# Batch 0's queries and keys loaded as bf16 from POOL's queue, and a new order of the opening

## The chip, the core and the metric

The kernel runs on one core of one Trainium2 chip. A core has a matrix engine (TensorE, PE in the profile, with its weight loads as PEld), a vector engine (VectorE, DVE), an activation engine (ScalarE, ACT), GpSimd (POOL) and a queue engine (SyncE, SP) that here only issues DMAs. POOL issues DMAs as well; the DMAs that it issues may change the type of the data on the way. Each engine runs its own instructions in order and waits for others by semaphores. Sixteen DMA engines serve all queues. SBUF is the on-chip memory of 128 partitions; PSUM holds TensorE's results.

The metric is the device time of one execution in microseconds (us), median over runs.

## The reference

Sliding-window attention (window 32 to each side) over 8 batches of 8 heads, 576 positions, head size 64, and then a two-layer network with a leaky ReLU over the 4608 tokens:

```python
scores = scale * np.matmul(q, k.transpose(0, 1, 3, 2))
mask = np.abs(pos[:, None] - pos[None, :]) <= window
scores = np.where(mask, scores, -1000000000.0)
scores = scores - np.max(scores, axis=-1, keepdims=True)
attn = np.exp(scores)
attn = attn / (np.sum(attn, axis=-1, keepdims=True) + 1e-09)
attn_out = np.matmul(attn, v)

x = attn_out.transpose(0, 2, 1, 3).reshape(B * S, H * D)   # 4608 x 512
h = x @ w_in                                               # 512 x 2048
out = np.maximum(0.01 * h, h) @ w_out                      # 2048 x 512
```

All inputs and the output are float32; the kernel computes in bf16 with float32 sums.

## The kernel before

The eight heads of a batch are taken in four pairs, a pair filling the 128 partitions with 2 x 64. A batch's 576 positions are two halves of 288. A *step* is one pair of one half: step i belongs to batch i // 8, half (i // 4) % 2 and pair i % 4.

For a step, `score(i)` (from line 270) multiplies the transposed queries `qT` with blocks of keys `kbd` on TensorE, five matmuls into the one PSUM tile `ps`; ACT takes the exponential `e`; POOL multiplies it with the window's mask into `prob` (line 282). `kbd` and `vbd` hold a pair's keys or values as block-diagonal tiles: the two heads of a pair stand on their own partitions, zero elsewhere, so these tiles have to be cleared once. `sums(i)` adds the probabilities with a matmul with `ones_bd` and takes the reciprocal on DVE (line 309). `product(i)` multiplies `prob` with `vbd` into the PSUM tile `x`, and `scaled(i)` writes `x` times the reciprocal into `xT` (DVE, line 334). `x` and the sums' tile `s` have one buffer each.

Once the four pairs of a half are in `xT`, the network's tiles run: `h_tile` (four matmuls over the 128-row slices c of `w_in`, line 348, and the leaky ReLU on ACT) and `o_tile` (sixteen matmuls with `w_out`, line 390). For the first half of batch 0, `h_first` runs the matmuls slice by slice, so that slice c waits only for pair c; its last part, c = 3, waits for `scaled(3)`. These matmuls are the dense stream that fills most of the span. From `h_tile(0, 4)` on the order is laid out by hand until the second half of batch 1 begins, and then by a fixed plan of due times. Every `step` of batch 1 needs `vbd` of batch 1, cast on ACT from `vf` (`cast_v`, line 203).

How queries and keys get transposed differs by batch. Batch 0 and 1: SP loads `qf` and `kf` as float32 (`load_qk`, line 79: 96 partitions, 6 positions in a row in each, both heads of the pair), an engine casts them to bf16 into `qb` and `kb` (`cast_qk`, lines 195 and 197; the tile holds both heads of a position side by side), TensorE transposes them in 6 matmuls for a pair (`transposes`, line 225), ACT evicts the PSUM tile `tp` into `qT` (line 233) or `kT` (line 239), and DVE copies `kT` into `kbd` in two halves (`place_keys`, line 258). Later batches are transposed by DMA.

The opening is one list of calls at the end of the kernel. Its queues are these:

- SP: all loads of batch 0 in the order q and k of pair 0, of pair 1, values of pair 0, q and k of pairs 2 and 3, values of pairs 1 to 3. After them come the loads of batch 1, whose first one waits for a POOL memset (line 75).
- POOL: the identity, the window (a memset and four selections), the clear of `vbd` of pair 3, then casts of keys, the masks, casts of values of pair 0, the probabilities, and the eight weight loads (`load_w_in`, line 448, and `load_w_out`, line 452: each reads 1 MB of float32 and writes 512 KB of bf16).
- DVE: cast of the identity, constants, the clear of `kbd` (line 134), then casts of queries, placing of keys, reciprocals and scalings.
- ACT: clears of `vbd` of pairs 0 to 2 (line 127), evictions, exponentials, the cast of the queries of pair 3, and the casts of values of pairs 1 to 3.
- TensorE: transposes of pairs 0 and 1, scores 0 and 1, sums 0, transposes of pair 2, product 0, and so on. `keep_busy` (line 402) puts matmuls in between whose result nobody reads.

Of the kernel before, what the change touches and what calls it, by code (L numbers as in the profile page):

```python
# [9 lines left out]
FP32 = mybir.dt.float32  # L10
BF16 = mybir.dt.bfloat16
AF = mybir.ActivationFunctionType
# [4 lines left out]
def kernel(  # L17
# [69 lines left out]
    def load_v(b, p):  # L87

        t = fload.tile([128, NB, D], FP32, name=f"vf{p}")
        for a in range(2):  # L90
            nc.sync.dma_start(  # L91
                out=t[64 * a:64 * a + 64],
                in_=v[b, 2 * p + a].rearrange("(c p) d -> p c d", p=64),
            )
        vf[b, p] = t

    load_qk(0, 0)
    load_qk(0, 1)
    load_v(0, 0)
    load_qk(0, 2)  # L100
    load_qk(0, 3)
    for p in range(1, NPAIR):
        load_v(0, p)


    ident_f = const.tile([128, 128], FP32)
    make_identity(nc, ident_f)
    ident = const.tile([128, 128], BF16)
    nc.vector.tensor_copy(out=ident, in_=ident_f)
# [7 lines left out]
    qb = const.tile([96, NPAIR, RUN, 2, D], BF16)  # L117
    kb = const.tile([96, NPAIR, RUN, 2, D], BF16)

    kbd = [const.tile([128, NPAIR, NB, 128], BF16, name=f"kbd{i}") for i in range(2)]  # L120
    vbd = [const.tile([128, NPAIR, NB, 128], BF16, name=f"vbd{i}") for i in range(2)]
    zero = const.tile([128, 1], BF16)
    nc.vector.memset(zero, 0.0)
# [10 lines left out]
    nc.vector.memset(kbd[0], 0.0)  # L134
    clear(vbd[0], 0)
    clear(vbd[0], 1)
    clear(vbd[0], 2)


# [6 lines left out]
    win = const.tile([128, 2, 3, 64], BF16)  # L146
    nc.gpsimd.memset(win, 1.0)
    for lo in (0, 64):
        w = win[lo:lo + 64]
        nc.gpsimd.affine_select(  # L150
            out=w, in_=w, compare_op=ALU.is_ge, fill=0.0,
            base=0, channel_multiplier=-1, pattern=[[1, 2], [0, 3], [2, 64]],
        )
        nc.gpsimd.affine_select(
            out=w, in_=w, compare_op=ALU.is_ge, fill=0.0,
            base=2 * W, channel_multiplier=1, pattern=[[-1, 2], [0, 3], [-2, 64]],
        )
    nc.gpsimd.memset(vbd[0][:, 3], 0.0)
# [16 lines left out]
    )  # L175

# [22 lines left out]
    def cast_v(b, p, on_act=False):  # L199
        for a in range(2):  # L200
            r = slice(64 * a, 64 * a + 64)
            if on_act:
                nc.scalar.activation(out=vbd[b % 2][r, p, :, r], in_=vf[b, p][r], func=AF.Copy)  # L203
            else:
                nc.gpsimd.tensor_copy(out=vbd[b % 2][r, p, :, r], in_=vf[b, p][r])  # L205
# [11 lines left out]

    def transposes(b):

        qT[b] = attn.tile([128, NPAIR, S], BF16, name="qT")  # L220
        for p in range(NPAIR):
            for which, src in (("q", qb), ("k", kb)):
                tp = mmps.tile([128, RUN, 96], BF16, name="tp", tag="mm")
                for c in range(RUN):
                    nc.tensor.transpose(  # L225
                        tp[:, c],
                        src[:, p, c].rearrange("p a d -> p (a d)"),
                        ident[0:96, 0:96],
                    )

                tok = tp.rearrange("p (e c) i -> p c i e", c=2)
                if which == "q":
                    nc.scalar.activation(
                        out=qT[b][:, p].rearrange("p (c i e) -> p c i e", c=2, e=RUN // 2),
                        in_=tok, func=AF.Copy,
                    )
                else:
                    kT = kt.tile([128, S], BF16, name="kT")
                    nc.scalar.activation(  # L239
                        out=kT.rearrange("p (i c) -> p i c", c=RUN),  # L240
                        in_=tp.rearrange("p c i -> p i c"), func=AF.Copy,
                    )
                    unplaced.append((b, p, kT))
                yield
# [50 lines left out]
    def sums(i):  # L295
# [3 lines left out]
        s = xps.tile([128, HALF], FP32, name="s")  # L299
# [154 lines left out]
    first = transposes(0)  # L454

    def first_pair():
        next(first)
        next(first)
        place_keys()

    cast_qk(0, 0, nc.vector)
    make_mask(0)
    cast_qk(0, 1, nc.vector)
    first_pair()
    first_pair()
    cast_v(0, 0)
    score(0)
    cast_qk(0, 2, nc.vector)
    score(1)
    sums(0)  # L470
    next(first)
    next(first)
    product(0)
    keep_busy(ps, 0, 2)
    place_keys()
    cast_qk(0, 3, nc.scalar)
    load_w_in(0, 512)
    scaled(0)
    sums(1)
    keep_busy(ps, 0, 3)  # L480
    load_w_in(512, 1024)
    load_w_in(1024, 1536)
    next(first)
    score(2)
    next(first)
    cast_v(0, 1, on_act=True)
    load_w_in(1536, 2048)
    make_mask(1)
    place_keys()
    keep_busy(ps, 0, 8)  # L490
    sums(2)
    score(3)
    load_w_out(0)
    product(1)
    scaled(1)
    cast_v(0, 2, on_act=True)
# [7 lines left out]
    cast_v(0, 3, on_act=True)  # L504
# [87 lines left out]
    def spend(us):  # L592
        nonlocal clock, turn
        while due and due[0] <= clock + 1e-6:
            due.pop(0)
            i = state["done"]
            if i < 11:
                cast_v(1, i - 7, on_act=True)
            step()
            if 10 <= i < 14:  # L600
                load_v(2, i - 10)
# [5 lines left out]
        if turn == 4:  # L607
            second_pair(3)
            cast_v(1, 0, on_act=True)
# [37 lines left out]
```

## Time and profile before

| what | value |
|---|---|
| median of 3 runs | 319.77 us (318.51 to 320.29) |
| span of the profiled execution | 318.5 us |
| TensorE busy | 303.2 us, 95% of the span |
| DVE, ACT, POOL busy | 218.2, 182.6, 191.6 us |
| TensorE busy from 0 to 25 us | 14.1 of 25.0 us |
| TensorE busy from 25 to 60 us | 33.8 of 35.0 us |
| TensorE busy from 60 us to the end | 255.3 of 258.5 us |
| granted TensorE clock in every stage | 1.00 |

The rows by stage are sums over windows of the span. The median of the runs lies 1.27 us above the span of the profiled execution. The next lines are what the profile shows of the loads of the first 50 us: what is loaded, from which queue, how often, the size written, and the median time from issue to landing.

```profile
qf<-in_q_dram SPq DMA_DIRECT2D x8, 288.0 KB, 7.9
kf<-in_k_dram SPq DMA_DIRECT2D x8, 288.0 KB, 8.9
w_in_bf<-in_moe_w_in_dram POOLq DMA_DIRECT2D x4, 512.0 KB, 8.6
w_out_bf<-in_moe_w_out_dram POOLq DMA_DIRECT2D x4, 512.0 KB, 16.8
vf<-in_v_dram SPq DMA_DIRECT2D x12, 144.0 KB, 8.2
```

### The profile page before, as it was taken

How to read it: one execution, taken by the hardware profiler on the slowest of the kernel's cores; microseconds unless marked ns; L12 is line 12 of the kernel's file. 1: busy time of each engine (PE TensorE's matmuls, PEld its weight loads, DVE VectorE, ACT ScalarE, POOL GpSimd, SP SyncE). 2: the span in 40 equal slices, each digit the busy share in tenths (PEclk: the TensorE clock that was granted, in tenths of full speed). 3: DMA queues.
4: the chain of work that ended last, by engine and by line, in shares of the span. 5: the costliest groups of instructions: out<-in, count | busy, mean ns of one | idle time of the engine just before them, and what ended most of it. 6: DMA issues, size and time to landing. Idle time of an engine off the chain costs nothing.

```text
span 318.5 us, 6474 instructions
## 1 busy us (share of the span) xinstructions
PE 303.2 (95%) x2449; PEld 204.3 (64%) x2449; DVE 218.2 (69%) x259; ACT 182.6 (57%) x393; POOL 191.6 (60%) x251
## 2 busy tenths in 40 slices
PE   2679998999999999999999999999999999999996
PEld 1467774585765858576765858576665858576653
DVE  5678955869655997688755997688745988565100
ACT  7577698474652828374652828375552837464531
POOL 7798963974546866686546866586637866330000
PEclk9999999999999999999999999999999999999999
DMA  8999999997999995399735995399733430000101
GB/s 179 211 186 218 267 250 203 250 206 181 216 242 196 231 206 150 82 251 203 155 76 127 238 227 136 75 223 232 162 76 104 109 70 33 35 35 2 66 31 71
DMA packets 108400, 49.46 MB, mean 155 GB/s; under 512 B 68816, under 2 KB 103888, under 8 KB 108368
## 3 DMA queue, kind: packets, MB, share of 16 engines
q1 hardware_dynamic: 104144, 44.84, 66.8%
q0 software_dynamic: 4224, 4.19, 8.0%
q8 instruction: 19, 0.31, 0.4%
q14 instruction: 13, 0.11, 0.1%
HBM read 36.70 MB, written 9.44 MB: 145 GB/s over the span
## 4 chain that ended last, share of the span: by engine, by line
PE 89%; DMA 3%; DVE 2%; SPq 1%; POOL 1%; ACT 1%; issue 1%; DVEq 0%; ACTq 0%
PE mm L348 39%; PE mm L390 38%; PE x L320 5%; PE ps L275 4%; DMA kf<-in_k_dram 3%; PE s L301 2%; DVE r L309 2%; SPq L79 1%; POOL w_in_bf L448 1%; DVE xT L334 1%; PE tp L225 1%; PE s L304 1%; ACT vbd L203 0%; SPq L91 0%; POOL prob L282 0%
## 5 line engine op out<-in xcount | busy, mean ns | idle before, releaser
L309 DVE RECIPROCAL r<-s 128x288 f32<-128x288 f32 x64 | 125.2, 1956 | 56.5 <-PE s L301 53.3
L282 POOL TENSOR_TENSOR prob<-e,mask 128x576 bf16<-128x576 bf16 x64 | 81.5, 1274 | 87.8 <-ACT e L280 41.1
L348 PE MATMUL mm<-xT,w_in_bf 128*128 128x288 bf16 x1024 | 134.0, 286 | 0.3
L390 PE MATMUL mm<-w_out_bf,gT 128*128 128x512 bf16 (+2 forms) x592 | 130.4, 373 | 0.2 <-DMA w_out_bf<-in_moe_w_out_dram 0.2
L355 ACT ACTIVATE gT<-mm 128x288 bf16<-128x288 f32 x256 | 101.4, 412 | 24.8 <-PE mm L348 8.5
L348 PEld LDWEIGHTS <-w_in_bf 128*128 128x128 bf16 x1024 | 98.4, 98 | 24.8 <-issue 0.6
L390 PEld LDWEIGHTS <-gT 128*128 128x128 bf16 x592 | 56.3, 98 | 59.6 <-issue 0.3
L395 ACT ACTIVATE o_sb<-mm 128x512 f32<-128x512 f32 (+2 forms) x37 | 21.7, 586 | 92.0 <-PE mm L390 92.0
L280 ACT ACTIVATE e<-ps 128x576 bf16<-128x576 f32 x64 | 41.4, 648 | 9.4 <-PE ps L275 9.2
L197 POOL CAST kb<-kf 96x384 bf16<-96x384 f32 (+1 forms) x56 | 35.5, 656 | 4.6 <-DMA kf<-in_k_dram 4.6
L205 POOL CAST vbd<-vf 64x576 bf16<-64x576 f32 x50 | 34.5, 689 | 1.8 <-DMA vf<-in_v_dram 0.4
L334 DVE TENSOR_TENSOR xT<-x,r 128x288 bf16<-128x288 f32 x64 | 29.3, 458 | 8.2 <-PE x L320 1.2
L260 DVE COPY kbd<-kT 64x576 bf16<-64x576 bf16 x48 | 32.3, 672 | 0.3
L275 PE MATMUL ps<-qT,kbd 128*128 128x128 bf16 (+2 forms) x320 | 26.5, 215 | 1.8 <-DVE kbd L258 1.2
L275 PEld LDWEIGHTS <-kbd 128*128 128x128 bf16 x320 | 21.0, 100 | 10.6 <-DVE kbd L258 1.5
L320 PE MATMUL x<-prob,vbd 128*128 128x128 bf16 (+2 forms) x320 | 26.0, 213 | 1.3 <-ACT vbd L203 0.7
L197 POOL CAST qb<-qf 96x384 bf16<-96x384 f32 x48 | 24.5, 538 | 0.0
L320 PEld LDWEIGHTS <-vbd 128*128 128x128 bf16 x320 | 20.6, 99 | 3.9 <-ACT vbd L203 1.8
L292 DVE TENSOR_TENSOR both<-prob 128x288 bf16<-128x288 bf16 x52 | 19.7, 380 | 0.9
L301 PE MATMUL s<-both,ones_bd 128*128 128x288 bf16 x52 | 14.9, 286 | 0.0
L258 DVE COPY kbd<-kT 64x576 bf16<-64x576 bf16 x16 | 7.1, 444 | 8.7 <-ACT kT L239 8.6
L225 PE MATMUL tp<-ident,qb 96*128 96x96 bf16 x48 | 4.4, 243 | 6.2 <-DVE qb L197 6.2
(43 smaller groups left out, 86.6 us busy)
## 6 DMA issues: line engine op xcount, KB each, us to landing
qf<-in_q_dram SPq DMA_DIRECT2D x32, 288.0 KB, 4.5
kf<-in_k_dram SPq DMA_DIRECT2D x32, 288.0 KB, 5.0
vf<-in_v_dram SPq DMA_DIRECT2D x64, 144.0 KB, 4.2
out_dram<-o_sb SPq DMA_DIRECT2D x35, 256.0 KB, 3.6
w_in_bf<-in_moe_w_in_dram POOLq DMA_DIRECT2D x4, 512.0 KB, 8.6
w_out_bf<-in_moe_w_out_dram POOLq DMA_DIRECT2D x4, 512.0 KB, 16.8
qT<-qb SPq DMA_TRANSPOSE x24, 4.1
kT<-kb SPq DMA_TRANSPOSE x24, 3.2
```

Source lines behind the costliest of these rows:

```text
L197: eng.tensor_copy(out=to, in_=tok)
L205: nc.gpsimd.tensor_copy(out=vbd[b % 2][r, p, :, r], in_=vf[b, p][r])
L260: nc.vector.tensor_copy(out=to.rearrange("p n (m c) -> p n c m", c=2), in_=kT[r].rearrange("p (c n m) -> p n c m", c=2, n=NB),)
L275: nc.tensor.matmul(ps_v[:, n_, :, i0:i0 + n], kbd[b % 2][:, p, blk], by_c[:, :, hf * EVEN + i0:hf * EVEN + i0 + n], start=True, stop=True,)
L280: nc.scalar.activation(out=e, in_=ps[:, P0:P0 + 2 * HALF], func=AF.Exp, scale=scale)
L282: nc.gpsimd.tensor_mul(pr.rearrange("p n c i -> p (n c i)"), e, mask[hf].rearrange("p n c i -> p (n c i)"),)
L309: nc.vector.reciprocal(r, s)
L320: nc.tensor.matmul(x_v[:, :, i0:i0 + n], vbd[b % 2][:, p, blk, :], pr[:, n_, :, i0:i0 + n], start=(blk == parts[0][1]), stop=(blk == parts ...
L334: nc.vector.tensor_mul(place(i), x, r)
L348: nc.tensor.matmul(h[:, 0:HALF], w_in_bf[:, c, ts(f, 128)], xT[:, c, ds(g * HALF % RING, HALF)], start=(c == 0), stop=(c == DMC - 1),)
L355: nc.scalar.activation(out=gT[:, f, ds(g * HALF % RING, HALF)].rearrange("p (i c) -> p i c", c=2), in_=h[:, 0:HALF].rearrange("p (c i) -> ...
L390: nc.tensor.matmul(o[:, lo:hi], gT[:, f, ds(128 * j % RING, 128)], w_out_bf[:, f, lo:hi], start=(f == 0), stop=(f == FFC - 1),)
```

## The change

Batch 0's queries and keys are no longer loaded by SP as float32 and cast. Six DMAs from POOL's queue write them as bf16: q and k of pair 0, of pair 1, and of pairs 2 and 3 together. The bf16 tile now holds each head's six positions in a row, so the transposes are made per head: 12 matmuls of 64 columns each for a pair's q or k, where there were 6 of 128. Batch 1 keeps the old way.

The keys of pairs 2 and 3 of batch 0 are evicted from PSUM straight into `kbd`, in two halves on ACT, without `kT` and DVE's copies.

The clears are dealt out anew: DVE clears `kbd` in two parts and `vbd` of pairs 1 to 3, ACT only `vbd` of pair 0. The window is made on 64 partitions (memset on DVE, two selections on POOL) and copied to the other 64 by DVE. The loads of batch 0's values wait for a small DVE memset. The list of calls of the opening has a new order: among other things transposes of q 2, q 3 and k 2 stand around sums 0, sums 1 use a buffer of the network's PSUM pool, one `w_in` load stands before probabilities 2 and two behind them, the first `w_out` load comes after the casts of values, and the cast of the values of pair 1 is split between ACT and DVE.

```diff
-    def load_v(b, p):
+    def load_v(b, p, behind=None):
 
         t = fload.tile([128, NB, D], FP32, name=f"vf{p}")
+        if behind is not None:
+            behind.memset(t[0:1, 0, 0:1], 0.0)
...
-    load_qk(0, 0)
-    load_qk(0, 1)
-    load_v(0, 0)
-    load_qk(0, 2)
-    load_qk(0, 3)
-    for p in range(1, NPAIR):
-        load_v(0, p)
...
+    def load_bf16(p, n):
+
+        for which, src in (("q", q), ("k", k)):
+            t = (qb if which == "q" else kb)[:, p:p + n].rearrange("p n c a d -> p (n c a d)")
+            t = t.rearrange("p (a c d) -> p a c d", c=RUN, d=D)
+            nc.gpsimd.dma_start(
+                out=t, in_=src[0, 2 * p:2 * (p + n)].rearrange("a (p c) d -> p a c d", c=RUN),
+            )
+            for i in range(n):
+                early[which, p + i] = t[:, 2 * i:2 * i + 2]
+
+    load_bf16(0, 1)
 
     ident_f = const.tile([128, 128], FP32)
     make_identity(nc, ident_f)
+    load_bf16(1, 1)
+    load_bf16(2, 2)
...
-    nc.vector.memset(kbd[0], 0.0)
-    clear(vbd[0], 0)
-    clear(vbd[0], 1)
-    clear(vbd[0], 2)
...
+    win = const.tile([128, 2, 3, 64], BF16)
+    nc.vector.memset(win[0:64], 1.0)
+    nc.vector.memset(kbd[0][:, 0:2], 0.0)
+    nc.vector.tensor_copy(out=ident, in_=ident_f)
+    for p in range(NPAIR):
+        load_v(0, p, nc.vector if p == 0 else None)
+    nc.vector.memset(kbd[0][:, 2:4], 0.0)
+    for p in range(1, NPAIR):
+        nc.vector.memset(vbd[0][:, p], 0.0)
...
+    def transpose(b, p, which):
+        tp = mmps.tile([128, RUN, 96], BF16, name="tp", tag="mm")
+        for c in range(RUN):
+            if b == 0:
+                for a in range(2):
+                    nc.tensor.transpose(tp[64 * a:64 * a + 64, c], early[which, p][:, a, c], ident[0:96, 0:96])
+            else:
+                src = (qb if which == "q" else kb)[:, p, c].rearrange("p a d -> p (a d)")
+                nc.tensor.transpose(tp[:, c], src, ident[0:96, 0:96])
+        return tp
+
+    def evict(b, p, which, tp, straight=False):
...
+        elif straight:
+
+            for a in range(2):
+                r = slice(64 * a, 64 * a + 64)
+                nc.scalar.activation(
+                    out=kbd[b % 2][r, p, :, r], in_=tp[r].rearrange("p c i -> p i c"), func=AF.Copy,
+                )
...
+    def turn_over(b, p, which, straight=False):
+        evict(b, p, which, transpose(b, p, which), straight)
...
-    def sums(i):
+    def sums(i, spare=False):
...
+        if spare:
+            s = mmps.tile([128, 512], FP32, name="mm", tag="mm")[:, 0:HALF]
+        else:
+            s = xps.tile([128, HALF], FP32, name="s")
...
-    cast_qk(0, 0, nc.vector)
+    qT[0] = attn.tile([128, NPAIR, S], BF16, name="qT")
+    turn_over(0, 0, "q")
+    turn_over(0, 0, "k")
+    turn_over(0, 1, "q")
+    place_keys()
+    nc.vector.tensor_copy(out=win[64:128], in_=win[0:64])
     make_mask(0)
-    cast_qk(0, 1, nc.vector)
-    first_pair()
-    first_pair()
+    turn_over(0, 1, "k")
+    score(0)
+    place_keys()
+    score(1)
+    turn_over(0, 2, "q")
+    tq3 = transpose(0, 3, "q")
+    sums(0)
+    turn_over(0, 2, "k", True)
+    evict(0, 3, "q", tq3)
+    place_keys()
+    tk3 = transpose(0, 3, "k")
+    keep_busy(ps, 0, 6)
+    sums(1, True)
     cast_v(0, 0)
-    score(0)
-    cast_qk(0, 2, nc.vector)
-    score(1)
-    sums(0)
-    next(first)
-    next(first)
+    load_w_in(0, 512)
+    score(2)
     product(0)
-    keep_busy(ps, 0, 2)
+    scaled(0)
+    evict(0, 3, "k", tk3, True)
+    keep_busy(ps, 0, 6)
+    cast_v(0, 1, nc.scalar, (0,))
+    cast_v(0, 1, nc.vector, (1,))
     place_keys()
-    cast_qk(0, 3, nc.scalar)
-    load_w_in(0, 512)
-    scaled(0)
-    sums(1)
-    keep_busy(ps, 0, 3)
     load_w_in(512, 1024)
     load_w_in(1024, 1536)
-    next(first)
-    score(2)
-    next(first)
-    cast_v(0, 1, on_act=True)
+    sums(2)
+    score(3)
+    product(1)
+    scaled(1)
     load_w_in(1536, 2048)
     make_mask(1)
-    place_keys()
-    keep_busy(ps, 0, 8)
-    sums(2)
-    score(3)
-    load_w_out(0)
-    product(1)
-    scaled(1)
-    cast_v(0, 2, on_act=True)
+    cast_v(0, 2, nc.scalar)
+    keep_busy(ps, 0, 6)
     score(4)
...
     sums(3)
-    cast_v(0, 3, on_act=True)
+    cast_v(0, 3, nc.scalar)
+    load_w_out(0)
     load_w_out(1)
```

## The prediction

> **What bounds the kernel now.** I read first the chain of waits of the whole span: TensorE holds 89% of it and the dense stream has no room. From the first dense matmul on, the change alters no line, so only the opening and what it hands on can move the end. The chain of the opening, part by part (start us, us, what):
>
> ```profile
> 5.83 9.66 DMA kf<-in_k_dram
> 15.49 0.05 issue
> 15.54 0.82 POOL kb L197
> 16.36 2.35 POOL w_in_bf L448 x3
> 18.72 0.01 issue
> 18.73 1.30 POOL prob L282
> 20.03 0.04 issue
> 20.07 0.42 PE s L304 x2
> 20.49 0.03 issue
> 20.52 1.97 DVE r L309
> ...
> 25.88 0.47 DVE xT L334
> 26.35 0.04 issue
> 26.39 0.65 PE mm L348 x4
> ```
>
> The last keys of batch 0 land at 15.49; POOL casts them, issues three weight loads, and only then multiplies probabilities 2; then VectorE's reciprocals run to 26.35. Second, the chain around 50 us, where the first product of batch 1 waits:
>
> ```profile
> 48.42 0.52 issue
> 48.95 0.20 ACT kT L239
> 49.14 0.47 issue
> 49.62 0.68 ACT vbd L203
> 50.30 0.03 issue
> 50.33 0.69 ACT vbd L203
> 51.02 0.05 issue
> 51.06 0.41 PE x L320 x5
> ```
>
> The reader is to see that the start of the dense stream isn't all: at 51.06 TensorE waits for two casts of batch 1's values. Third, the DMA issues with their times to landing: the first values of batch 1 are issued at 32.46 and 34.36 and take 16.6 and 15.3 us, so they land at 49.06 and 49.66. The last part of w_out is issued at 29.88 and takes 18.9 us: 48.8, where the timeline shows TensorE released by it. Fourth, the timeline of POOL, because line 75's memset opens batch 1's loads on SP's queue:
>
> ```profile
> 24.92 0.80 POOL L452 DMA_DIRECT2D w_out_bf<-in_moe_w_out_dram  x1
> 25.72 0.09 POOL L75 MEMSET qf<- 1x1 f32 x1
> ```
>
> and the first and last slow TensorE work:
>
> ```profile
> 12.78 0.64 PE L304 MATMUL s<-prob,ones_bd 128*128 128x288 bf16 x2 [0.37 <-POOL prob L282]
> ...
> 18.45 1.25 PE L402 MATMUL ps<-mask,ones_bd 128*128 128x224 bf16 x8 [0.35 <-ACT e L280]
> ```
>
> Early on six transposes take 0.66 us (0.11 each); around 42 us twelve take 0.51 (0.043 each). The change of pace lies inside the row at 18.45, near 19.1: 6.3 us after the stretch without long gaps began at 12.78.
>
> **The change, part by part.** All times below are from the span's start.
>
> *Removed.* Eight q and k issues on SP (0.40 to 0.80 each), three casts on DVE (3.0 us in all), one on ACT (0.83), four on POOL (3.75 in all); from POOL also the window's memset and two of four selections (0.42 + 2 x 0.54), and the 1.06 us clear; from ACT two clears (2 x 1.09); for pairs 2 and 3 the kT evictions and four DVE copies (4 x 0.45). Of this POOL's casts lie on the opening's chain; DVE's and ACT's mostly don't.
>
> *POOL's six loads.* Its eight later weight loads cost 0.75 to 0.93 each, so I take 0.8: two from 0.81 to 2.4, identity work (0.50) to 2.9, four more to 6.1. The two selections then end at 7.2, and the mask waits for DVE's copy of the window. Nothing on POOL is wanted before the first probabilities, at 11: these 4.8 us are covered; without that cover they'd be 4.8 on the chain. The price of landing isn't in the trace for a cast of this size. Below: SP's first 288 KB load took 3.4. Above: the shortest w_in load, reading 1 MB, took 5.5. The size is the former's, so I take 3.6: q of pair 0 lands at 4.4. For the rest: side by side, from 32 to 46 us, SP's loads came 1.69 us per 288 KB, and w_out's parts (1 MB read) about 4.6 us apart, 1.3 us per 288 KB read. By that pair 1 lands at 6.8 and 8.1, q of pairs 2 and 3 at 10.7, k at 13.3; at the pace of the SP queue alone (last k at 15.49) some 2 us later.
>
> The Trainium skill, page "SBUF — State Buffer", section "Who interferes with whom", speaks against this: while DVE runs a copy in a two-port mode, GpSimd can't write descriptors. The row: three weight issues took 2.41 us while DVE ran the scaling and a reciprocal, no longer than the others. Here DVE runs memsets and one cast of the identity (0.41 in the trace); by the rule the sum grows by at most 0.4, by the row by nothing.
>
> *Values.* SP's four pairs now wait for a DVE memset, after about 2.4 us of DVE work: issue from 3.2, against 2.74. With the longest early landing (6.7) pair 0 is there at 10, and its POOL cast comes at 13.9: covered by 4 us. SP has nothing else queued behind it until batch 1.
>
> *TensorE.* 48 more transposes. The first 48 stand ahead of score 0: 48 x 0.11 = 5.3, from 4.4 to 9.7, and the landings keep ahead. Score 0 takes 0.65 to 10.35; ACT evicts the k of pair 1 until 10.45, so the exponential ends at 11.15 and probabilities 0 run on POOL 11.15 to 12.4 (before: 11.46). DVE's copies of pair 1 (0.91) end at 11.4; score 1 and its exponential end at 12.6, probabilities 1 at 13.9. By the clock row (6.3 us of steady work: 10.7) the next 24 transposes, of q 2 and q 3, cost 24 x 0.045 = 1.1: to 12.95, sums 0 to 13.2. If it stayed slow they'd cost 2.6.
>
> The skill's page "TensorE: Matmul & The Clock Gate", section "Part 1: The HAM clock gate", gives about 3.4 us of sustained work before full clock. The trace's 6.3 is longer. By the rule the last of the first 48 would be quick, some 0.9 us would go from the opening and the sum would be 317.4.
>
> *DVE, what sets the dense start.* From 13.25: four reciprocals 7.8, four scalings 1.84, the value cast put there 0.66 (as ACT's or POOL's for that shape), two waits of 0.25 for products: 23.8 to 24.1, against 26.35. So the dense stream may start 2.3 us earlier. The cast of the other half on ACT, and pairs 2 and 3 there (1.39 each), stand where they stood.
>
> *POOL, what sets the arrivals.* k of pair 2 is transposed to 13.8, evicted in two halves of 0.65 and followed by q 3's eviction (15.85) and exponential 2 (16.5). Probabilities 2: 16.5 to 17.8. Then back to back two w_in loads 1.6, probabilities 3 1.27, w_in 0.8, the mask 0.84, probabilities 4 1.27, two w_out loads 1.6: 7.4, and line 75's memset comes at 25.2: only 0.5 before its old 25.72. The first w_in load goes out at 15.2 rather than 16.31, 1.1 earlier, with the values out of its way. Batch 1's queue and the weights share the DMA until 49, so arrivals come 0.5 to 1.1 earlier; I take 0.8.
>
> *Sum.* At 51.06 the dense stream would be early by 2.3, but the second half of the values lands at 49.66 - 0.8; plus its cast 0.69 and hand-over 0.05 the product starts at 49.6. That is 1.45 earlier: the 0.65 that stood between landing and cast, and 0.8. About 0.85 of the earlier start is given back as a wait. Behind 51 the order and work are unchanged, so the 1.45 goes through: span 318.5 - 1.45 = 317.05. The runs' median, 319.77, lies 1.27 above that span; on it: **318.3**, with 317.3 to 319.2 as this case's own range (arrivals 0 to 1.8 earlier).
>
> **Rivals.**
>
> *A. The whole earlier start goes through.* Then 2.3, and up to 0.9 more were the last 14 of the first 48 transposes quick (14 x 0.067): 316.6 to 317.5, say 317.0. For it: the opening's 3.5 MB now come over two queues, which between 32 and 46 us read together some 400 GB/s where SP's alone moved 200. Against: POOL's 7.4 us back to back, which no quicker landing shortens.
>
> *B. Hidden anyway.* If line 75 comes no earlier and the weights' backlog stays, only part of the 0.65 is left: 319.5. For it: the two loads moved behind probabilities 2. Against: three kb casts less before it.
>
> *C. Slower: the last keys come late.* Place: transposes of k 2, before sums 1 and score 2 in TensorE's order. Price: landing at 15.5 as SP's did, with slow transposes (1.3), moves probabilities 2 to 19.5 and line 75 to 28.2; batch 1 arrives 2.45 later, less the 0.65: 1.8 slower, 321.6. It takes the gain away from a landing at 14.7 on. For it: six software loads, the last issued at 6, beside the values' 256-byte pieces on SP's queue. Against: the shared pace of 32 to 46 us, which gives 13.3.
>
> **How the numbers follow.** Forecast 0.42, A 0.27, B 0.10, C 0.21. This kernel's runs tell about 0.5%, 1.6 us. The forecast's own range straddles 318.17: 0.18 beyond it, 0.24 within. Faster: 0.27 + 0.18 = 0.45; same 0.24 + 0.10 = 0.34; slower 0.21. The range leaves a tenth at each end: 316.6 (A's far end) to 321.2 (most of the way to C).
>
> **What would show it.** Right: q of pair 0 landing near 4.4, score 0 near 9.7, the first reciprocal near 13.2, line 75 near 25.2, the first matmul of the last w_in slice near 24, and a new TensorE wait on the last w_out part or on batch 1's values near 47 to 50. Wrong: transposes waiting for the software loads; slow transposes after 11; the wait near 50 unchanged in length, which is A. The sum fails most easily at the 0.8, which rests on a shared DMA, and at the clock.

## The result and the profile after

| | kernel before | changed kernel |
|---|---|---|
| median of 6 runs | 319.30 us (318.51 to 320.29) | 321.69 us (320.25 to 322.18) |
| ratio of the times | 1 | 1.0061, 95% interval 1.0038 to 1.0083 |
| time and span of the profiled execution | 320.29, 318.5 | 322.18, 320.5 |
| last keys of batch 0 landed | 15.49 | 14.56 |
| probabilities 2 start | 18.73 | 18.86 |
| memset that opens batch 1's loads (line 75) | 25.72 | 27.26 |
| first matmul of the last `w_in` slice | 26.39 | 26.69 |
| last part of `w_out` landed | 48.80 | 50.69 |
| first pair of batch 1's values landed | 49.11, 49.70 | 51.07, 51.65 |
| first product of batch 1 | 51.06 | 52.60 |
| end of the span, counted from that product | 267.44 | 267.88 |

All positions are us from the start of the span, read from the trace of one execution. The changed kernel is 0.6% slower: 2.4 us by the medians, 2.0 by the two profiled spans. Of these 2.0, 1.54 are there at the first product of batch 1, and 0.44 come after the last eviction; in between, the two kernels run at a constant distance. Runs more than 1.5% above the fastest of their kernel are left out of the ratios in this document; only *held_feed* below has such runs, 6 of its 12.

One execution is a weak witness for less than a microsecond. Four kernels of the last experiment run, up to the first product of batch 1, the code of the kernel before (two of them) or of the changed kernel (the other two). That product is at 51.06, 49.96 and 50.40 in the three traces of the old opening, and at 52.60, 51.01 and 52.90 in those of the new one: on average 1.7 later, with over 1 us between executions of the same opening. So below, the ratios of many runs decide, and a position decides only where many traces agree.

The chain of waits through the opening of the changed kernel (start us, us, what):

```profile
4.03 5.92 DMA kb<-in_k_dram
...
9.99 0.71 PE tp L232 x12
...
12.37 0.64 PE ps L299 x5
13.01 1.10 PE tp L232 x14
14.11 0.59 PE s L331 x2
14.70 1.10 PE tp L232 x24
15.80 1.23 PE ps L429 x6
17.03 0.48 PE mm L331 x2
...
18.86 1.26 POOL prob L306
20.13 1.50 POOL w_in_bf L475 x2
...
25.80 1.48 POOL w_out_bf L479 x2
27.28 0.08 POOL qf L75
27.36 0.02 issue
27.38 8.29 DMA qf<-in_q_dram
35.67 0.02 issue
35.68 15.39 DMA vf<-in_v_dram
```

The reader is to see three things. The keys of pair 1 land only at 9.95, and everything behind them shifts; the last keys, landed at 14.56, kept nobody waiting here. Between probabilities 2 and line 75 POOL works without a gap for 8.4 us. And the chain then no longer goes through TensorE: from line 75 on it is two DMAs, the second a load of values that takes 15.4 us. It ends here (same view, near 50 us):

```profile
51.15 0.69 ACT vbd L212
51.84 0.03 issue
51.86 0.69 ACT vbd L212
52.55 0.05 issue
52.60 0.41 PE x L347 x5
```

Who waited for whom, TensorE alone, from 26 to 56 us (in total, times, longest); first the kernel before, then the changed one:

```profile
PE x L320 <- ACT vbd L203: 0.7, 1, 0.7
PE mm L390 <- DMA w_out_bf<-in_moe_w_out_dram: 0.2, 1, 0.2
```

```profile
PE tp L235 <- POOL kb L205: 0.8, 2, 0.6
PE mm L417 <- DMA w_out_bf<-in_moe_w_out_dram: 0.7, 1, 0.7
PE x L347 <- ACT vbd L212: 0.4, 1, 0.4
```

The dense stream starts only 0.3 later than before (26.69 against 26.39). Of the other 1.2 of the 1.54, 1.0 are these waits: 1.9 us instead of 0.9, each for something that came by DMA (batch 1's keys, the weights, batch 1's values). The remaining 0.2 is in no wait of the list.

The six new loads in the view of the changed kernel's first 15 us of DMA (number, KB written, median us from issue to landing):

```profile
qb<-in_q_dram POOLq DMA_DIRECT2D x2, 144.0 KB, 4.4
kb<-in_k_dram POOLq DMA_DIRECT2D x2, 144.0 KB, 4.6
qb<-in_q_dram POOLq DMA_DIRECT2D x1, 288.0 KB, 7.9
kb<-in_k_dram POOLq DMA_DIRECT2D x1, 288.0 KB, 9.2
```

And the stretch from 15 to 20 us, first the kernel before, then the changed one (length; busy us and number of PE, PEld, DVE, ACT, POOL; TensorE clock, DMA share, GB/s):

```profile
15.00:20.00 5.00, 4.25 (x32) 3.17 (x31) 4.38 (x7) 3.73 (x7) 4.50 (x7) 1.00 1.26 170
```

```profile
15.00:20.00 5.00, 4.24 (x44) 3.38 (x41) 4.11 (x3) 3.84 (x7) 3.20 (x5) 1.00 0.71 105
```

The DMA engines, full before, are not full now: three weight loads were on their way by 18 us before, one is now, and batch 0's loads have nearly run out.

### The profile page after: what moved, and what is told of

It is laid out like the page before. It is cut to its first block, busy times and chain, and to the rows that moved or that the text cites. A ratio compares the mean times of both kernels' runs of the same rounds, so it can differ in the third digit from the quotient of the medians.

```text
span 320.5 us, 6551 instructions
## 1 busy us (share of the span) xinstructions
PE 303.0 (95%) x2482; PEld 205.2 (64%) x2502; DVE 216.3 (67%) x260; ACT 180.6 (56%) x391; POOL 188.6 (59%) x249
## 4 chain that ended last, share of the span: by engine, by line
PE 83%; DMA 9%; POOL 3%; DVE 1%; issue 1%; ACT 1%; ACTq 0%; POOLq 0%; DVEq 0%
PE mm L417 37%; PE mm L375 34%; DMA vf<-in_v_dram 5%; PE ps L299 4%; PE x L347 4%; DMA qf<-in_q_dram 3%; PE s L328 2%; DMA kb<-in_k_dram 2%; POOL prob L306 1%; PE tp L232 1%; POOL w_in_bf L475 1%; DVE r L336 1%; POOL w_out_bf L479 0%; ACT vbd L212 0%; PE ps L429 0%
## 5 line engine op out<-in xcount | busy, mean ns | idle before, releaser
L336 DVE RECIPROCAL r<-s 128x288 f32<-128x288 f32 x63 | 123.2, 1956 | 58.7 <-PE s L328 53.6
L417 PE MATMUL mm<-w_out_bf,gT 128*128 128x512 bf16 (+2 forms) x572 | 128.7, 373 | 1.7 <-DMA w_out_bf<-in_moe_w_out_dram 0.7
L304 ACT ACTIVATE e<-ps 128x576 bf16<-128x576 f32 x64 | 41.5, 648 | 10.5 <-PE ps L299 10.4
L205 POOL CAST kb<-kf 96x384 bf16<-96x384 f32 (+1 forms) x52 | 30.7, 613 | 5.3 <-DMA kf<-in_k_dram 5.3
L284 DVE COPY kbd<-kT 64x576 bf16<-64x576 bf16 x48 | 32.3, 673 | 0.3
L282 DVE COPY kbd<-kT 64x576 bf16<-64x576 bf16 x12 | 5.4, 446 | 6.8 <-ACT kT L253 4.8
L232 PE MATMUL tp<-ident,qb 96*64 96x96 bf16 x48 | 2.5, 282 | 7.5 <-DMA qb<-in_q_dram 7.5
```

What stands on the lines that cost most here:

```text
L205: eng.tensor_copy(out=to, in_=tok)
L284: nc.vector.tensor_copy(out=to.rearrange("p n (m c) -> p n c m", c=2), in_=kT[r].rearrange("p (c n m) -> p n c m", c=2, n=NB),)
L304: nc.scalar.activation(out=e, in_=ps[:, P0:P0 + 2 * HALF], func=AF.Exp, scale=scale)
L336: nc.vector.reciprocal(r, s)
L417: nc.tensor.matmul(o[:, lo:hi], gT[:, f, ds(128 * j % RING, 128)], w_out_bf[:, f, lo:hi], start=(f == 0), stop=(f == FFC - 1),)
```

## The experiments

In each, `prob 2` is the start of probabilities 2, `open` the memset of line 75, and the ratio is to the kernel before, run beside it, with its 95% interval.

### The order of POOL's weight loads

*weights_early*: the changed kernel with its second and third `w_in` loads where the kernel before has them.

```diff
     load_w_in(0, 512)
+    load_w_in(512, 1024)
+    load_w_in(1024, 1536)
     score(2)
...
-    load_w_in(512, 1024)
-    load_w_in(1024, 1536)
     sums(2)
```

> The changed kernel with the second and third w_in load moved ahead of probabilities 2 on POOL, nothing else. Theory G (the gate: batch 1's loads open behind line 75's memset, and the end follows their arrival): probabilities 3 still wait for their exponential, so line 75 stays at 27.2 (27.0 to 27.4), the first product of batch 1 at 52.6, and the time at the changed kernel's, 1.006 of the one before. Rival W (the weights' backlog: the last part of w_out lands late, 50.7): the software queue starts some 3 us earlier with these two, so the last part lands 1 to 2 earlier and the product comes at 51 to 51.6, 1.002 of the one before.

Measured: 1.006 (1.0038 to 1.0082). Prob 2 at 17.98, open at 26.37, product of batch 1 at 51.67, 0.93 sooner than in the changed kernel; but this profiled execution lost 1.5 us again between 116 and 126 us, on a chain that starts from a transposing load of later keys, 4.5 us long. By the median nothing was won: inconclusive by itself.

*before_order*: that, and the fourth `w_in` load, the first `w_out` load and the second mask as before too.

```diff
-    load_w_in(512, 1024)
-    load_w_in(1024, 1536)
+    load_w_in(1536, 2048)
+    make_mask(1)
     sums(2)
...
-    load_w_in(1536, 2048)
-    make_mask(1)
...
+    load_w_out(0)
     score(4)
...
-    load_w_out(0)
     load_w_out(1)
```

> As weights_early, and the fourth w_in load and the second mask ahead of probabilities 3, the first w_out load ahead of probabilities 4: POOL's order of the kernel before, from the first w_in load on. G: probabilities 3 at 21.6 as now, line 75 at 25.7 (1.5 earlier), the first product of batch 1 at 51.1, 1.000 to 1.002 of the kernel before. Rival L (late landings of batch 0's queries and keys set the loss, POOL's order doesn't): no earlier than the changed kernel by more than 0.4 us, 1.005 or more.

Measured: 1.0022 (1.0007 to 1.0038); open at 26.04, last `w_out` landed at 48.86, as before. The new order of POOL's list costs about 0.4% of the 0.6%. The edit moves two things, the weight loads and line 75, so it doesn't say which of them counts. In its profile, the slowest of its 12 runs, the first product of batch 1 was at 52.31 all the same, though the first values had landed at 49.22: pair 1's keys came at 10.45, the latest of all traces, and the dense stream itself was late (first matmul of the last `w_in` slice at 27.16).

*before_late*: the reverse, the kernel before with two weight loads behind probabilities 2.

```diff
-    load_w_in(512, 1024)
-    load_w_in(1024, 1536)
     next(first)
     score(2)
+    load_w_in(512, 1024)
+    load_w_in(1024, 1536)
```

> The kernel before with its second and third w_in load moved behind probabilities 2, nothing else. G: probabilities 2 at 18.4, probabilities 3 at 22.9, line 75 at 27.1 rather than 25.7, the first product of batch 1 at 52.4, 1.004 of the kernel before. Rival L: with nothing late in the landings it stays within 0.2% of the kernel before.

Measured: 1.0046 (1.0026 to 1.0066). The second and third `w_in` load went out at 19.2 and 20.0 instead of 17.2 and 18.0, open was at 26.31 against 25.72, and the kernel got slower. Prob 2, at 18.02, gained nothing by it: it waited for its exponential, and the two other traces of the old opening, with the loads ahead of it, have it at 17.62 and 18.09. Later weight loads are a loss, and nothing was bought with it.

The traces agree. From the issue of the first `w_in` load to the landing of the last part of `w_out` it is 32.0 to 33.3 us in the seven traces with POOL's old order of the weights (before, old_open_349, old_open_339, before_order, held_order, ident_held, ident_order), and 33.3 to 35.6 in the seven with the second and third load behind probabilities 2 (after, new_open_349, new_open_339, values_held, no_warm_six, by_copy, before_late). Weights_early, between the two orders, has 34.3; gate_early and extra_load put other loads in between and don't count here.

### The values beside the queries and keys

*values_held*: the changed kernel with SP's loads of batch 0's values behind one more DVE memset, 3 us later.

```diff
-    for p in range(NPAIR):
-        load_v(0, p, nc.vector if p == 0 else None)
     nc.vector.memset(kbd[0][:, 2:4], 0.0)
     for p in range(1, NPAIR):
         nc.vector.memset(vbd[0][:, p], 0.0)
+    for p in range(NPAIR):
+        load_v(0, p, nc.vector if p == 0 else None)
```

> The changed kernel with the loads of batch 0's values opened by the same DVE memset, but behind the clears of vbd, at about 6.8 us rather than 3.7. If the values' pieces on SP's queue are what delays the software loads: q of pair 1 lands at about 7 (now 8.9), k at 8 (now 9.95), k of pairs 2 and 3 at 12 to 13 (now 14.6); probabilities 0 at 10.3 and probabilities 2 at 17.3 (now 18.9), line 75 1 to 1.5 earlier, 1.001 to 1.003 of the kernel before. If the software loads are slow by themselves: q of pair 1 within 0.4 of 8.9, and the time that of the changed kernel.

Measured: 1.0025 (1.0008 to 1.0043). The DMA issues of its first 15 us, to be held against the four lines above:

```profile
qb<-in_q_dram POOLq DMA_DIRECT2D x2, 144.0 KB, 3.5
kb<-in_k_dram POOLq DMA_DIRECT2D x2, 144.0 KB, 3.5
qb<-in_q_dram POOLq DMA_DIRECT2D x1, 288.0 KB, 6.0
kb<-in_k_dram POOLq DMA_DIRECT2D x1, 288.0 KB, 7.0
```

With the values 3 us later, pair 1's keys land at 7.92 instead of 9.95 and the last keys at 12.39 instead of 14.56; prob 2 is at 16.84 and open at 25.25, each 2.0 sooner. This holds in every trace: pair 1's keys land at 7.9 to 8.6 in the six with the values held, at 9.0 to 10.5 in the eight of the new opening without, on average 1.3 us later. So it was the values that held the six loads up. But the product of batch 1 comes only 0.8 sooner (51.80), behind a longer wait for `w_out`:

```profile
PE mm L417 <- DMA w_out_bf<-in_moe_w_out_dram: 2.8, 2, 1.8
```

*held_order*: both edits, that of values_held and that of before_order.

> values_held and before_order together. Theory D (the end follows the later of two things: the start of the dense stream, and the landing of batch 1's values, which comes when the DMA engines have moved all that stands before them, so any time in which they lack work between 15 and 20 us is paid at 50): probabilities 2 at 16.9, last w_in slice's first matmul at 24.6 (as values_held), three w_in loads out by 16.8, first values of batch 1 landing at 48.2 to 49 (before 49.06, changed 51.08, values_held 50.24), first product of batch 1 at 49.8 to 50.5, 0.996 to 0.999 of the kernel before. Rival (the DMA is full from 16 us on whatever the order, the landing stays): values at 50 or later, product at 51.5 or later, 1.001 or more.

Measured: 1.0011 (0.9993 to 1.0029), no difference from the kernel before, where 0.996 to 0.999 was expected. Open at 24.88 and the last keys sooner than in either kernel, but `w_out` landed at 48.99 and the product came at 50.88, after 1.0 us of waiting for `w_out`. The two edits alone win 0.39% and 0.36%, together 0.50%. The intervals don't tell 0.50 from their sum; that something else ends last from there on is read from that wait.

*held_feed*: held_order with the first two weight loads still earlier, so that they fill DMA time before 18 us.

```diff
     score(0)
+    load_w_in(0, 512)
     place_keys()
     score(1)
+    load_w_in(512, 1024)
     turn_over(0, 2, "q")
...
-    load_w_in(0, 512)
-    load_w_in(512, 1024)
```

> held_order with the first w_in load between probabilities 0 and 1, the second ahead of the casts of values: 11.4 and 13.5 rather than 14.4 and 15.2. D: the engines have work without a gap, batch 1's values land at 47 to 48.3, the wait at the first product of batch 1 nearly goes and the dense start decides: product at 49.2 to 50, 0.993 to 0.998. Rival: as held_order within 0.1%, or slower because the weights delay the values of pair 0 (their cast later than 15).

Measured: 1.0102 (1.0070 to 1.0135), slower where 0.993 to 0.998 was expected. The profiled execution took 330.46, above the six that the ratio goes by (320.81 to 324.50). In it the weights overtook batch 0's values: the last four of their eight loads, issued from 10.7 to 15.2, landed at 20.9, 24.7, 28.4 and 32.1, and TensorE waited for their casts, once for 5.5 us; the granted clock was then 0.50 from 31.0 to 37.9. That the same wait, shorter, makes the 1.0102 isn't shown, since none of those six was profiled. The DMA view from 16 to 34 us has the last of the loads, 16.9 us for 144 KB:

```profile
vf<-in_v_dram SPq DMA_DIRECT2D x1, 144.0 KB, 16.9
```

One such load (147 KB in pieces of 256 bytes) landed every 3.7 us, 40 GB/s, while the weights (pieces of 2 KB, written as 1 KB) were read at 1.05 MB in 3.2 us, 328 GB/s: a ratio of 8.2, where the pieces have 8. The DMA view from 21 to 25 us counts about as many pieces of the one as of the other (queue: pieces, MB written, share; q0 has the weights, q1 the values):

```profile
q0 software_dynamic: 634, 0.63, 92.8%
q1 hardware_dynamic: 619, 0.15, 29.1%
```

It is no fixed rule. In the changed kernel from 6 to 9 us, with six new loads (pieces of 1.5 KB, written as 768 bytes) beside the values, it was 2.3 to 1:

```profile
q0 software_dynamic: 447, 0.32, 76.3%
q1 hardware_dynamic: 1035, 0.26, 46.5%
```

### Single parts of the new opening

*no_warm_six*: without the six matmuls that nobody reads, ahead of sums 1.

```diff
     tk3 = transpose(0, 3, "k")
-    keep_busy(ps, 0, 6)
     sums(1, True)
```

> The changed kernel without the six keep_busy matmuls ahead of sums 1. If they stand on the opening's chain (1.23 us at the slow pace, ahead of sums 1 and score 2): probabilities 2 start 3.9 us after probabilities 1 rather than 5.1 (then ACT's evictions limit), line 75 about 0.7 to 1.2 earlier against probabilities 0, 1.002 to 1.005 of the kernel before. Rival (they buy the fast pace): the pace change comes after 19.5 rather than near 19, sums and products behind it slow, no gain: 1.006 or more.

Measured: 1.0059 (1.0035 to 1.0083), the changed kernel's own ratio; open at 27.47, prob 2 at 18.63, only 0.2 sooner. This doesn't show that the 1.23 us in the chain above are free. In this execution the last keys landed at 14.97 and TensorE waited 0.65 for them; and the change to the fast pace, which the trace's records of the clock put at 19.0 in the changed kernel, came at 20.9, so that sums 2 and score 3 took 0.64 each instead of 0.40. The six delay score 2 and bring the fast pace sooner, as the rival had it; here the two cancelled.

*by_copy*: keys of pairs 2 and 3 through `kT` and DVE's copies again.

```diff
-    turn_over(0, 2, "k", True)
+    turn_over(0, 2, "k")
...
-    evict(0, 3, "k", tk3, True)
+    evict(0, 3, "k", tk3)
```

> The changed kernel with the keys of pairs 2 and 3 taken the old way: evicted whole to kT by ACT, placed by DVE. DVE is in reciprocal 0 when k of pair 2 is evicted, so its copies end 1 to 1.5 us later than ACT's second half does now: score 2, probabilities 2 and line 75 1 us later, 1.008 to 1.010 of the kernel before. Rival (ACT is freed by 0.65 per pair and this decides): probabilities 2 no later, 1.006 or less.

Measured: 1.0123 (1.0088 to 1.0159). Open at 29.20 and the product at 54.60, 1.9 and 2.0 later than in the changed kernel. The straight eviction is a real gain, 0.6%. Part of it can be the clock: the profile grants 0.50 from 22.9 to 26.3, and the run with the best mean clock, 0.998, took 323.05, where the median is 323.61. From the fourth `w_in` load to line 75 POOL's list moved by 1.9, and the product moved with it.

### What ends last near 50 us

*gate_early*: held_order with line 75's memset and batch 1's loads right behind the last `w_in` load.

```diff
     load_w_in(1536, 2048)
+    for p in range(NPAIR):
+        load_qk(1, p, nc.gpsimd if p == 0 else None)
+    for p in range(NPAIR):
+        load_v(1, p)
     make_mask(1)
...
-    for p in range(NPAIR):
-        load_qk(1, p, nc.gpsimd if p == 0 else None)
-    for p in range(NPAIR):
-        load_v(1, p)
```

> held_order with line 75's memset and the loads of batch 1 opened right behind the fourth w_in load, about 5 us sooner (near 20 rather than 24.9). Theory F (a floor: from 16 to 49 us the DMA engines are full, and what stands before batch 1's values takes until 49 whatever the order): the queries of batch 1 land earlier, but the weights later in turn; last part of w_out and first values of batch 1 both land within 0.7 of held_order's 48.95 and 49.38, first product within 0.6 of 50.9, time within 0.3% of held_order. Rival G (the gate sets it): values land 3 to 5 us sooner, product at 49.5 or before, 0.996 or less.

Measured: 1.0112 (1.0071 to 1.0153). The profile is of the fastest of the four runs, 320.93; the two slowest, 324.41 and 324.91, have a mean clock of 0.995 and 0.992. Open at 19.24, 5.6 sooner than in held_order. Batch 1's first values landed at 43.8 and 47.6 instead of 49.4 and 49.7, which theory F didn't allow; `w_out` still landed at 48.96, the product came at 51.37, not sooner, and TensorE got a new wait, for the last part of `w_in`, which landed at 32.6 instead of 29.8:

```profile
PE mm L375 <- DMA w_in_bf<-in_moe_w_in_dram: 1.5, 1, 1.5
```

*extra_load*: held_order with one more load of 1 MB, that nobody reads, behind line 75.

```diff
+    extra = const.tile([128, DMC, 512], BF16)
...
+    def load_extra():
+        nc.gpsimd.dma_start(out=extra, in_=w_in_r[:, :, 0:512])
...
+    load_extra()
```

> held_order with one more load of 1 MB (a copy of the first w_in slice into a tile that nobody reads), issued by POOL right behind line 75's memset. F: 1.05 MB at the 400 GB/s that both queues read together is 2.6 us: last part of w_out 2.3 to 3 later, first product of batch 1 at 53 to 54, 1.008 to 1.011 of the kernel before. Rival G: only POOL's 0.8 us count, the product by at most 51.5, 1.003 or less.

Measured: 1.0164 (1.0143 to 1.0184), 4.9 us above held_order by the ratios, where some 2 to 3 were expected; the last part of `w_out` landed at 51.37, 2.4 later, and the product of batch 1 came at 53.97, 3.1 later. Its chain and its waits from 26 to 56 us, and the busy times from 51.5 to 54.9 (the number 0.50 is the granted TensorE clock):

```profile
28.82 22.54 DMA w_out_bf<-in_moe_w_out_dram
```

```profile
PE mm L417 <- DMA w_out_bf<-in_moe_w_out_dram: 3.7, 2, 2.1
```

```profile
51.50:54.90 3.40, 3.40 (x18) 1.87 (x18) 0.69 (x1) 2.25 (x4) 0.00 (x0) 0.50 1.14 205
```

A megabyte that nobody waits for moved the landing of `w_out` by more than the change did (2.4 against 1.9). The rest of the 4.9 comes with a slower clock: behind the wait it was halved for 3.4 us, and the four runs have mean clocks of 0.989 to 0.994, where those of held_order have 0.998 to 1.000. So the bytes that must pass until 50 us, and the DMA time left unused before 20 us, are what I take to set the end there; starting batch 1's loads sooner (gate_early) took from `w_in` what it gave to the values.

### POOL's start

*ident_held* and *ident_order*: held_order and before_order with POOL's identity work ahead of the six loads.

```diff
-    load_bf16(0, 1)
-
     ident_f = const.tile([128, 128], FP32)
     make_identity(nc, ident_f)
+    load_bf16(0, 1)
+
     load_bf16(1, 1)
```

> held_order with the identity made ahead of POOL's six loads. It takes the 0.5 us gap out between the second and the third load: q of pair 1 0.3 to 0.6 sooner, if the first load isn't moved back by as much (it now starts at 1.38, the identity ends at 1.4 in the kernel before). F: probabilities 2 and the dense start 0.3 to 0.6 sooner, but the first product still at 50.4 or later: within 0.2% of held_order. Rival G or a dense start that decides: product sooner by the same 0.3 to 0.6, 0.998 to 1.000 of the kernel before.

> before_order (values not held) with the identity ahead of the loads. There the dense start is the later one (first product at 52.3 with values landed at 49.2): 0.3 to 0.6 sooner landings of pair 1 give a product 0.3 to 0.6 sooner, 1.000 to 1.002 of the kernel before. Rival: the values' pieces take what the gap gave up, no change, 1.002 or more.

Measured: 1.0025 (1.0010 to 1.0039) and 1.0033 (1.0021 to 1.0046). In both, the first load was issued at 1.58 instead of 1.38, the third at 3.03 instead of 3.37; against 1.0011 and 1.0022 nothing that the intervals tell apart.

### The last half microsecond

From the end of the last eviction to the end of the span it is 2.74 us in the kernel before and 2.73 in before_late, but 3.16 to 3.19 in the twelve others that have the new opening and all their stores, though in all of them the last output has landed 1.6 after that eviction. In this stretch SP's program ends with waits for its DMAs and three instructions that the trace calls DRAIN. SP's program has 349 instructions in the trace of before and 339 in that of the changed kernel (eight loads fewer and two waits). So four kernels were made, two with the old opening and two with the new one, one of each two with 349 instructions and one with 339. In all four the 48 DMA transposes of batches 2 to 7 are plain DMAs of equal size, and 3 to 14 output stores are left out, by which SP's number of instructions is set; times are therefore not compared, only this stretch. Three kernels that keep the transposes and change the length alone (after_ten_more, held_ten_more, before_ten_less) have no result. The edit of new_open_339:

```diff
-            nc.sync.dma_start_transpose(
-                out=t.rearrange("p (c i) -> p c i", c=RUN),
-                in_=src[:, p].rearrange("p c a d -> p (c a d)"),
-            )
+            nc.sync.dma_start(out=t, in_=w_in_bf[:, 0, 0:S])
...
-            nc.sync.dma_start(out=out[ts(j, 128), lo:hi], in_=o_sb[:, lo:hi])
+            parts = 0 if j in range(10, 18) else 2 if j in range(26, 26) else 1
+            for r in range(parts):
...
```

> The kernel before, with the 48 DMA transposes of batches 2 to 7 replaced by plain DMAs of the same target size from SBUF (so queries and keys of these batches are not computed), and with nine output stores left out and one split in two, so that SP's program should have 349 instructions in the trace, as the kernel before has. Theory (the length of SP's program sets the end): from the end of the last eviction to the end of the span 2.74 us, as before. Rival (the end goes with the opening): 2.74 too. This is the base of the four.

> As old_open_349, with five more output stores left out, so that SP's program should have 339 instructions, as the changed kernel has. Theory of SP's program length: 3.1 to 3.2 us from the last eviction to the end of the span, with the old opening. Rival (the end goes with the opening): 2.74.

> The changed kernel, with the 48 DMA transposes of batches 2 to 7 replaced in the same way and three output stores left out, so that SP's program should have 349 instructions. Theory of SP's program length: 2.74 us from the last eviction to the end of the span, with the new opening. Rival (the end goes with the opening): 3.1 to 3.2.

> As new_open_349, with five more output stores left out, so that SP's program should have 339 instructions, as the changed kernel has. Theory of SP's program length: 3.1 to 3.2 us from the last eviction to the end of the span. Rival (the end goes with the opening): 3.1 to 3.2 too. If all four show one number, something that the replaced transposes took away sets the end.

Measured: 2.76, 3.01, 2.97 and 3.15 us, so neither theory alone: the length adds 0.25 and 0.18, the opening 0.21 and 0.14. SP's drains by line, number, and ns (shortest/median/longest), in old_open_349, old_open_339, new_open_349 and new_open_339:

```profile
L645 SPq DRAIN  x3: 7/7/7, 316.6 to 316.9; - x3
```

```profile
L645 SPq DRAIN  x3: 7/7/130, 316.9 to 317.6; - x3
```

```profile
L670 SPq DRAIN  x3: 7/7/7, 317.8 to 318.1; - x3
```

```profile
L670 SPq DRAIN  x3: 7/7/130, 319.5 to 320.2; - x3
```

The reader is to see the longest: 130 ns at 339 and 7 at 349, whichever the opening. From the end of the first drain to the end of the second it is 0.47 at 339 and 0.06 at 349, in both openings; from the end of the first drain to the end of the span it is 1.24 and 1.25 at 339, 0.83 and 0.84 at 349. So this stall of 0.41 us goes with the length of SP's program. In the changed kernel the longest is 130 ns as well and the first of the two stretches 0.50, in the kernel before 7 ns and 0.07. The totals don't follow the length alone, since the first drain itself comes at 1.76 to 2.13: SP waits for its DMAs in a fixed list, two to an instruction, and in these traces each that stands behind the one that lands last costs another 0.06. In the kernels before and after the first drain is at the same place (1.90 and 1.89), so that there the stall is all of the 0.44. Why it depends on the length wasn't tried. The trace has an 8 KB instruction load nearby; at 339 it starts 1.0 us behind the first drain, when the second has already ended, and before the drains at 349.

## Why the prediction failed

It said 318.3 and faster; it is 321.69, slower and outside the range, and closest to rival C (321.6).

**The step that failed** is "Batch 1's queue and the weights share the DMA until 49, so arrivals come 0.5 to 1.1 earlier; I take 0.8." Batch 1's values came 2.0 later instead (51.07 against 49.11), and the last part of `w_out` 1.9 later. Two terms were wrong in it.

- *Line 75 "comes at 25.2".* It came at 27.26. POOL's list from prob 2 to line 75 was priced rightly (8.7, measured 8.4). Prob 2 was not: 18.86, not 16.5. The larger part was there when the transposes of k 2 began, at 14.63 instead of 13.2: pair 1's keys landed at 9.95 instead of 8.1, because SP's values took their share of the DMA engines (with the values held back prob 2 came at 16.84), and POOL's first load was issued 0.6 later than assumed (1.38, not 0.81). The other 0.9 came behind them, where the sum let ACT's evictions decide: the six unread matmuls and sums 1 stood ahead of score 2 at the slow pace.
- *The weights.* I counted the first weight load as 1.1 earlier and "the two loads moved behind probabilities 2" as rival B's small matter. In fact the first went out at 16.32, as before, and the second to fourth at 20.1 to 22.9, 2.8 to 2.9 later than before; the DMA engines ran short of work from 17 to 20 us (105 GB/s instead of 170 from 15 to 20). Before_order shows 0.4% for the order of POOL's list. That it works through the issue of the weights, and not through line 75, is argued from gate_early, where line 75 came 5.6 sooner and the product didn't.

**Removed and added work.** The prices on TensorE were below the estimate: 12 transposes of 64 columns took 0.69 us, 0.06 each instead of the 0.11 that was taken from 128 columns; ahead of score 0 TensorE waited for landings, up to 2.8 us, and not for the clock. Score 0 came at 10.61 instead of 9.7.

**The clock.** I let the change of pace come 6.3 us behind the first transposes, at 10.7. It came at 19.0 by the trace's records of the clock, since the first transposes stood apart by waits of up to 2.8 us; counted from 12.37, where the stretch without long gaps begins, it is 6.6. The 24 transposes at 12.94 took 1.17 us, by luck near the 1.1 I had: they ran at the slow pace, at a lower price than the slow one I took.

**The dense start.** "23.8 to 24.1" was 26.69: it hangs on the same late keys. And rival A, that a sooner start goes through, is not borne out by held_order: its products of steps 4 to 7 come 0.63 sooner than in the kernel before, the first of batch 1 only 0.18 sooner.

**Rival C** had the right sign; that its 321.6 is so near is luck. It priced last keys that land at 15.5 and keep the transposes of k 2 waiting. They landed at 14.56, and TensorE didn't wait for them; pair 1's keys were what came late. Its own sum was uneven, too: the 14.7 from which the gain was to be gone is near what quick transposes give (14.6), while with the slow ones of its price it would be 13.7, and a landing at 14.56 would then cost 0.9 us and not 2.4. It lacked the weights, and 0.44 of the time it gave was found at the end of the program. Early keys alone don't mend the kernel (values_held, 1.0025).

**The sum** set the median 1.27 above the profiled span. Over six runs of the kernel before it is 0.8, as the profiled execution was its slowest; that would lower the forecast and explains nothing of the miss. The 0.44 at the end of the program no step had.

The pieces of the profiled difference of 2.0, as shown: a later dense start 0.3, longer waits for DMA near 50 us 1.0 (and 0.2 there that no wait shows), the stall between SP's drains 0.44.

## What to carry to other kernels

When the DMA engines are full from one point of the program to another, count the bytes that have to pass and the start of the first loads: here sooner work between the two points bought little (held_order, gate_early), and weight loads moved behind other work in POOL's order cost 0.4% (before_order, before_late). What is wanted first should have the engines to itself: keys that ran beside the values came 1.3 us later on average (values_held), and values in small pieces beside weights in large ones fell far behind in the one trace that shows it (held_feed). Before a gain in the opening is carried through to the end, ask what arrives last at the next stage, and what has to be undone for it. And before a shift of 1 us between two traces is explained, look at how far two traces of the same code lie apart: here up to 1.9 us.

## What the hardware showed

- Queues shared the DMA engines by pieces rather than by bytes: 256-byte pieces beside 2 KB pieces got an eighth (40 against 328 GB/s in held_feed), with 619 pieces to 634 from 21 to 25 us. The Trainium skill, page "DMA: Bandwidth & Descriptors", section "Queues, rings and completion order", says that each DMA engine goes round its queues packet by packet, a packet being several descriptors. The ratio of 8.2 agrees with turns that hold equally many pieces on both sides; the changed kernel's 1035 to 447 from 6 to 9 us does not.
- POOL's first load was issued 0.67 us after POOL was ready for it, SP's at 0.82 against POOL's 1.38; it took 0.83 us to issue, each further one 0.63 to 0.68.
- The first record of TensorE's clock, at full speed, is at 19.2 us in the kernel before, 19.0 in the changed one, 17.3 in values_held, 15.6 in gate_early and 20.9 in no_warm_six, and the matmuls change pace there; the 1.00 that the windows ahead of it show stands for no record. Counted from where steady work began it is 6.4 (from 12.78), 6.6 (from 12.37), 6.9 (from 10.35), 4.7 (from 10.90) and 8.8 (from 12.04, with a wait of 0.65 inside). The page "TensorE: Matmul & The Clock Gate", section "Part 1: The HAM clock gate", gives about 3.4 of sustained work, watched in a window that runs free of the kernel; by it full clock would come 3.4 to 6.8 us after steady work begins, which is an estimate. Four of the five agree with that to 0.1; the fifth, with the wait inside, is longer. The stretches between two changes of the clock in these traces are whole multiples of 3.41 us.
- Behind waits for `w_out` of 3.7 us in all, the longest 2.1, the granted clock was 0.50 for 3.4 us (extra_load).
- Ten instructions fewer in SP's program made its end stall for 0.41 us, in both openings; by the total the end was 0.18 to 0.25 us longer.
